# Attention and gated feed-forward on one core: weights and v as casting transfers, smaller opening loads, a first weight block done unit by unit

## The chip, the cores and the metric

The kernel runs on one core of one Trainium2 chip. The metric is the device time of one execution in microseconds (us). A profile comes from one single execution of a kernel, and its span is some 1.8 us shorter than the device time of that execution.

## The reference, cut to what matters

```python
def _attn_ref(q, k, v):                    # 8 x 8 x 576 x 64, float32
    rel = pos[:, None] - pos[None, :]
    mask = (rel >= 0) & (rel < 64)         # each query sees itself and 63 keys before it
    scores = np.where(mask, q @ k^T / sqrt(64), -1e9)
    return softmax(scores) @ v

def _moe_ref(x, w_gate, w_val, w_out):     # 4608 x 512; 512 x 1536 twice; 1536 x 512
    return (np.maximum(x @ w_gate, 0) * (x @ w_val)) @ w_out
```

x is the attention's output, 4608 tokens of 512 values. The kernel cuts the tokens into 24 **units** of 192 (three to a batch) and into 12 **tiles** of two units each. A tile goes through w_gate and w_val (the matmuls called h, in 12 column groups f = 0 to 11 each) and then through w_out (the matmuls called op). The weights are cut into three **blocks**: gate 0, 1, 2 and value 0, 1, 2, each 512 x 512, or 1 MB in float32. Block 0 serves f = 0 to 3, block 1 f = 4 to 7, block 2 f = 8 to 11.

## The kernel before

All inputs come as float32 and are computed in fp16. Before, the loads go through the sync engine's queue into float32 buffers (half of batch 0's q and k go through ScalarE's queue, before the change and after it), and GpSimd casts them in SBUF:

```python
def w_load(wt, src, j, at):
    ...
    stg = stage.tile([128, 2, 512], FP32, name="stg")
    nc.sync.dma_start(stg, part)
    def cast():
        nc.gpsimd.tensor_copy(dst, stg)
        w_done.add((wt.name, j))
    W.at(at, cast)

def v_load(u):
    ...
    nc.sync.dma_start(vn[p0:128, w], v[b, :, k0 + p0:k0 + 128].rearrange("h p d -> p h d"))

def u_cast(u, name):          # k, q and v of one unit; q of unit 0 on ScalarE, the rest on GpSimd
    ...
    nc.gpsimd.tensor_copy(c16, src)
```

`W` is a list of pieces of work with planned times; it decides only the order in which instructions are written to each engine. At run time every engine takes its own instructions in that order and waits on semaphores. The steps of one unit, in its own names:

```python
def u_exp(u, g):   ... nc.scalar.activation(p, st, ACT.Exp, scale=scale)            # ScalarE
def u_mask(u, g):  ... nc.vector.tensor_tensor(p, p, mask.to_broadcast(...), MUL)   # VectorE, two SBUF inputs
def u_copy(u, g):  ... nc.scalar.copy(d["xs"][:, g], d["pv"][g])                    # ScalarE
def u_norm(u):     ... nc.vector.tensor_tensor(xt[...], d["xs"][:, :, 0], rs, MUL)  # writes one unit's half of xt
```

The main program:

```python
        qk_load(0)                        # q and k of batch 0: units 0, 1 and 2
        ...
        W.advance(22.0)
        heat = f_ps.tile([128, 512], FP32, name="heat", tag="h")
        for _ in range(14): ...           # matmuls whose result nobody reads, to warm the clock
        ...
        ready(2)                          # units 0 and 1 normalised
        hidden(0, 0, TT)                  # h of tile 0, both units at once: 384 columns a matmul
        ready(3)
        hidden(1, 0, U)                   # h of tile 1, first unit
        output_by_rows(0)
        ...
```

The softmax here doesn't subtract the row's maximum and nothing guards it: scores larger than these inputs give would overflow.

## Time and profile before

| | before |
|---|---|
| device time, median of 3 (lowest to highest) | 362.14 us (361.67 to 362.98) |
| first h matmul | 31.93 us |
| first group that needs value block 2 (f = 8) | 45.74 us |
| first op matmul | 58.71 us |
| TensorE busy between 100 and 350 us | 249.2 of 250 us |

The table is to be read from the bottom. From about 60 us on TensorE is full, so the program's end is the moment at which that full stretch begins, plus a constant. All that moving loads and casts can gain lies in the first 60 us. I use the third row as a milestone: the start of the first h group that needs value block 2. The profile's lines that carry this stand in the prediction below, except the milestone's own:

```profile
45.74 0.81 PE L341 MATMUL h<-xt,wv 128*128 128x384 f16 x4
```

### The profile page before, as it was taken

The numbers are of one execution on the slowest core, as the hardware profiler recorded it, in microseconds if no ns is written. First come the engines' busy times: TensorE is split into PE (matmuls) and PEld (weight loads), VectorE is DVE, ScalarE is ACT, GpSimd is POOL, SyncE is SP. The second block draws the span as 40 slices with busy tenths as digits, with TensorE's granted clock in tenths as the row PEclk, the third lists the DMA queues.
The fourth block names the chain that finished last, engine by engine and source line by source line (L and its number), as shares of the span: only waits on it lengthen the run. The fifth ranks groups of instructions, "written<-read, shape, count | busy, mean of one in ns | idle before, by whom it ended". The sixth has DMA issues, their size and how long they took to land.

```text
span 360.2 us, 8167 instructions
## 1 busy us (share of the span) xinstructions
PE 333.6 (93%) x3230; PEld 196.6 (55%) x3230; DVE 238.2 (66%) x450; ACT 179.4 (50%) x387; POOL 94.7 (26%) x114
## 2 busy tenths in 40 slices
PE   0276999999999999999999999999999999999995
PEld 0253676685664664664664654654664664654652
DVE  0799747887785785776776776776686686684330
ACT  1362544674663663662662662652752752762421
POOL 2678633408115111025105210025105201000000
PEclk9998999999999999999999999999999999999999
DMA  8999948996991701991991701991992701001002
GB/s 191 262 340 388 321 122 192 208 240 152 211 183 61 148 0 60 211 184 59 217 181 59 147 2 58 204 189 64 194 195 68 147 2 58 31 2 59 31 1 87
DMA packets 94215, 49.82 MB, mean 138 GB/s; under 512 B 48096, under 2 KB 84960, under 8 KB 94176
## 3 DMA queue, kind: packets, MB, share of 16 engines
q1 hardware_dynamic: 91808, 48.12, 61.1%
q10 hardware_dynamic: 2368, 1.18, 1.5%
q8 instruction: 25, 0.41, 0.5%
q14 instruction: 14, 0.11, 0.1%
HBM read 39.85 MB, written 9.44 MB: 137 GB/s over the span
## 4 chain that ended last, share of the span: by engine, by line
PE 86%; DVE 8%; DMA 3%; ACT 1%; issue 1%; ACTq 0%; DVEq 0%
PE h L341 51%; PE op L355 25%; PE pv L253 6%; PE st L226 3%; DMA qn<-in_q_dram 3%; DVE p L242 2%; DVE xt L285 1%; DVE rs L279 1%; DVE g_sb L331 1%; DVE sT L271 1%; DVE qT L212 1%; ACT xs L266 0%; ACTq L164 0%; DVE kT L212 0%; DVE rT L273 0%
## 5 line engine op out<-in xcount | busy, mean ns | idle before, releaser
L341 PE MATMUL h<-xt,wg 128*128 128x384 f16 (+1 forms) x624 | 120.4, 316 | 3.7 <-DVE xt L285 3.5
L341 PE MATMUL h<-xt,wv 128*128 128x384 f16 (+1 forms) x624 | 120.1, 316 | 0.4 <-DVE g_sb L331 0.4
L331 DVE TENSOR_TENSOR g_sb<-r_sb,h 128x384 f16<-128x384 f32 (+1 forms) x156 | 79.1, 512 | 61.9 <-PE h L341 55.0
L328 ACT ACTIVATE r_sb<-h 128x384 f32<-128x384 f32 (+1 forms) x156 | 73.5, 472 | 77.1 <-PE h L341 53.0
L355 PE MATMUL op<-wo,g_sb 128*128 128x512 f16 x432 | 95.7, 380 | 0.0
L341 PEld LDWEIGHTS <-wg 128*128 128x128 f16 x624 | 58.8, 98 | 40.0 <-POOL wv L134 3.3
L341 PEld LDWEIGHTS <-wv 128*128 128x128 f16 x624 | 58.5, 98 | 34.7 <-issue 1.1
L355 PEld LDWEIGHTS <-g_sb 128*128 128x128 f16 x432 | 41.8, 98 | 48.9
L242 DVE TENSOR_TENSOR p<-p,mask 128x512 f16<-128x512 f16 x96 | 46.2, 503 | 30.3 <-ACT p L238 29.4
L238 ACT ACTIVATE p<-st 128x512 f16<-128x512 f32 x96 | 52.7, 611 | 9.6 <-PE st L226 9.2
L362 ACT COPY o_sb<-op 128x512 f32<-128x512 f32 x36 | 20.9, 586 | 68.6 <-PE op L355 68.6
L266 ACT COPY xs<-pv 128x384 f32<-128x384 f32 x96 | 40.2, 496 | 10.9 <-PE pv L253 10.9
L200 POOL CAST k<-kn 128x768 f16<-128x768 f32 x24 | 23.8, 992 | 77.0 <-DMA kn<-in_k_dram 44.1
L200 POOL CAST q<-qn 128x768 f16<-128x768 f32 x23 | 19.4, 843 | 56.4 <-DMA qn<-in_q_dram 42.0
L212 DVE STREAM_TRANSPOSE kT<-k 128x384 f16<-128x384 f16 x48 | 27.8, 590 | 9.0 <-POOL k L200 7.7
L193 POOL CAST v<-vn 128x1024 f16<-128x1024 f32 x16 | 16.8, 1051 | 61.7 <-PE pv L253 49.5
L226 PE MATMUL st<-qT,kT 32*128 32x128 f16 x768 | 16.9, 227 | 15.5 <-DVE qT L212 15.5
L253 PE MATMUL pv<-p,v 128*64 128x128 f16 x384 | 25.0, 229 | 3.5 <-DVE p L242 3.3
L212 DVE STREAM_TRANSPOSE qT<-q 128x384 f16<-128x384 f16 x48 | 26.5, 581 | 1.7 <-ACT q L198 1.5
L271 DVE STREAM_TRANSPOSE sT<-xs 128x768 f32<-128x768 f32 x24 | 22.7, 948 | 6.1 <-ACT xs L266 6.1
L226 PEld LDWEIGHTS <-kT 32*128 32x128 f16 x768 | 12.3, 98 | 23.3 <-issue 11.3
L253 PE MATMUL pv<-p,ones 128*64 128x128 f16 x384 | 24.5, 227 | 0.0
(28 smaller groups left out, 132.7 us busy)
## 6 DMA issues: line engine op xcount, KB each, us to landing
vn<-in_v_dram SPq DMA_DIRECT2D x40, 256.0 KB, 5.1
out_dram<-o_sb SPq DMA_DIRECT2D x36, 256.0 KB, 2.0
kn<-in_k_dram SPq DMA_DIRECT2D x26, 288.0 KB, 6.2
qn<-in_q_dram SPq DMA_DIRECT2D x26, 288.0 KB, 9.2
stg<-in_moe_w_gate_dram SPq DMA_DIRECT2D x6, 512.0 KB, 7.3
stg<-in_moe_w_val_dram SPq DMA_DIRECT2D x6, 512.0 KB, 7.0
stg<-in_moe_w_out_dram SPq DMA_DIRECT2D x6, 512.0 KB, 7.3
vn<-in_v_dram SPq DMA_DIRECT2D x8, 128.0 KB, 8.4
```

The lines of the kernel that those rows point to most:

```text
L200: nc.gpsimd.tensor_copy(c16, src)
L212: nc.vector.transpose(dst.rearrange("p h (m i j) -> p h m j i", i=32, j=2), src)
L226: nc.tensor.matmul(d["st"][g][:, (2 * hh + w) * 128:(2 * hh + w + 1) * 128], kT[rows, dh, hh, ks + 128 * w:ks + 128 * w + 128], d["qT"][ro ...
L238: nc.scalar.activation(d["p"][g].rearrange("p h c -> p (h c)"), d["st"][g], ACT.Exp, scale=scale)
L242: nc.vector.tensor_tensor(p, p, mask.rearrange("p w c -> p (w c)")[:, None, :].to_broadcast([128, 2, 256]), MUL)
L253: nc.tensor.matmul(pv[64 * e:64 * e + 64, s, 64 * w:64 * w + 128], d["v16"][:, w, 2 * g + e] if s == 0 else (ones0 if u % UB == 0 and w == ...
L266: nc.scalar.copy(d["xs"][:, g], d["pv"][g])
L271: nc.vector.transpose(sT.rearrange("p g b c -> p g (b c)"), d["xs"][:, :, 1])
L328: nc.scalar.activation(r_sb[:, 0:n], h1[:, 0:n], ACT.Relu)
L331: nc.vector.tensor_tensor(g_sb[:, f, c0:c1], r_sb[:, 0:n], h2[:, 0:n], MUL)
L341: nc.tensor.matmul(h[:, 0:n], wt[:, c, f * 128:f * 128 + 128], xt[:, c, c0:c1], start=(c == 0), stop=(c == NC - 1))
L355: nc.tensor.matmul(op, g_sb[:, f, bass.ds(sub * 128, 128)], wo[:, f], start=(f == 0), stop=(f == NF - 1))
```

## The change

Its intent is to get TensorE going earlier. It has three parts, which I call a, b and c.

- **a** Weights and v are cast on their way in. A transfer issued from GpSimd reads float32 and writes fp16. The float32 buffers and GpSimd's casts of weights and v go away; GpSimd now issues those transfers instead. The sync engine's queue keeps q, k and the outputs.
- **b** The opening loads of q and k cover units 0 and 1 only; unit 2's part follows later.
- **c** Weight block 0 is applied to unit 0 as soon as that is ready, then to unit 1 (192 columns a matmul), and only from f = 4 on to both at once. The heating matmuls are gone.

```diff
-        stg = stage.tile([128, 2, 512], FP32, name="stg")
-        nc.sync.dma_start(stg, part)
-        def cast(): nc.gpsimd.tensor_copy(dst, stg) ...
+        nc.gpsimd.dma_start(dst, part)                      # a: casts on the way
 ...
-            nc.sync.dma_start(vn[p0:128, w], v[b, ...])
+            nc.gpsimd.dma_start(v16[p0:128, w], v[b, ...])  # a
 ...
-        qk_load(0)
+        qk_load(0, (0, 6), "k", True)                       # b: units 0 and 1
+        qk_load(0, (0, 6), "q", True)
 ...
+        W.at(6.5, lambda: v_load(0))
+        W.at(9.8, lambda: v_load(1))
+        cols = [(wt, src, j) for j in range(3) for wt, src in ((wg, moe_w_gate), (wv, moe_w_val))]
+        rows = [(wo, moe_w_out, j) for j in range(3)]
+        for c, t in zip(cols + rows, (8.0, 12.0, 16.0, 19.0, 25.0, 28.0, 34.0, 37.0, 40.0)):
+            W.at(t, lambda c=c: w_load(*c))
+        W.at(9.0, lambda: qk_load(0, (6, 9)))               # b: unit 2
+        W.at(22.0, lambda: v_load(2))
+        W.at(31.0, lambda: qk_load(1, (0, 3)))
 ...
+        plan_unit(2, 26.0, (16.0, 17.0), ...)               # unit 2's k and q casts on GpSimd
 ...
-        for _ in range(14): ... heat ...
-        hidden(0, 0, TT)
+        ready(1)
+        hidden(0, 0, U, 0, 4)                               # c
+        ready(2)
+        hidden(0, U, TT, 0, 4)
+        hidden(0, 0, TT, 4)
```

(Cut: plan times of the other units, helper arguments, the casts of unit 0's k and unit 1's q moved from GpSimd to ScalarE, and the weights' transfers, which read 1 MB each instead of 512 KB.)

More of the change, by code (lines that the diff above doesn't have):

```diff
@@ L70 @@
     persist = ctx.enter_context(tc.tile_pool(name="persist", bufs=1))
-    stage = ctx.enter_context(tc.tile_pool(name="stage", bufs=6))
     a_in = ctx.enter_context(tc.tile_pool(name="a_in", bufs=2))
@@ L120, with w_load @@
     w_done = set()
-    def w_load(wt, src, j, at):
+    def w_load(wt, src, j):
         sr = src.rearrange("(c p) n -> p c n", p=128)
         if wt is wo:
-            dst, part = wo[:, 2 * j:2 * j + 2], sr[:, 2 * j:2 * j + 2]
+            dst, part = wo[:, 4 * j:4 * j + 4], sr[:, 4 * j:4 * j + 4]
         else:
-            cs, ns = slice(2 * (j % 2), 2 * (j % 2) + 2), slice(512 * (j // 2), 512 * (j // 2) + 512)
-            dst, part = wt[:, cs, ns], sr[:, cs, ns]
-        stg = stage.tile([128, 2, 512], FP32, name="stg")
-        nc.sync.dma_start(stg, part)
-        def cast():
-            nc.gpsimd.tensor_copy(dst, stg)
-            w_done.add((wt.name, j))
-        W.at(at, cast)
+            ns = slice(512 * j, 512 * j + 512)
+            dst, part = wt[:, :, ns], sr[:, :, ns]
+        nc.gpsimd.dma_start(dst, part)
+        w_done.add((wt.name, j))
     def w_need(wt, f):
-        j = f // 2 if wt is wo else 2 * (f // 4) + 1
-        while (wt.name, j) not in w_done:
+        while (wt.name, f // 4) not in w_done:
             W.pop()
-    def queue(b, g):
-        return nc.scalar if b == 0 and g >= G // 2 else nc.sync
     def qk_tiles(b):
@@ L154, in qk_tiles, with qk_load @@
                 units[UB * b + i][name + "nat"] = nat
-    def qk_load(b, blocks=None):
+    def qk_load(b, blocks=None, names="kq", two=False):
         for name, src in (("k", k), ("q", q)):
+            if name not in names:
+                continue
             nat = units[UB * b + UB - 1][name + "nat"].rearrange("p h u m e -> p h (u m) e")
@@ L162, in qk_load @@
                 rows = slice(32 * g, 32 * g + 32)
+                eng = nc.scalar if two and g >= G // 2 else nc.sync
                 if blocks is None:
-                    queue(b, g).dma_start(
+                    eng.dma_start(
                         nat[rows].rearrange("p h m e -> p (h m) e"),
@@ L169, in qk_load @@
                     for h in range(2):
-                        queue(b, g).dma_start(
+                        eng.dma_start(
                             nat[rows, h, m0:m1],
@@ L177, in v_load @@
         d = units[u]
-        vn = d["v"] = a_in.tile([128, 2, H, 64], FP32, name="vn", bufs=3)
+        v16 = d["v16"] = a_16.tile([128, 2, H, 64], FP16, name="v16", bufs=3)
+        if u == 0:
+            nc.vector.memset(v16[0:64, 0], 0.0)
+        elif uu == 0:
+            nc.gpsimd.memset(v16[0:64, 0], 0.0)
         for w in range(2):
@@ L181, in v_load @@
             p0 = max(0, -k0)
-            nc.sync.dma_start(vn[p0:128, w], v[b, :, k0 + p0:k0 + 128].rearrange("h p d -> p h d"))
+            nc.gpsimd.dma_start(v16[p0:128, w], v[b, :, k0 + p0:k0 + 128].rearrange("h p d -> p h d"))
     def u_cast(u, name):
         d = units[u]
-        if name == "v":
-            v16 = d["v16"] = a_16.tile([128, 2, H, 64], FP16, name="v16")
-            if u % UB == 0:
-                nc.gpsimd.memset(v16[0:64, 0], 0.0)
-                nc.gpsimd.tensor_copy(v16[64:128, 0], d["v"][64:128, 0])
-                nc.gpsimd.tensor_copy(v16[:, 1], d["v"][:, 1])
-            else:
-                nc.gpsimd.tensor_copy(v16, d["v"])
-        else:
-            c16 = d[name + "16"] = a_16.tile([128, 2, 3, 128], FP16, name=name + "16")
-            src = d[name]
-            if name == "q" and u == 0:
-                nc.scalar.copy(c16, src)
-            else:
-                nc.gpsimd.tensor_copy(c16, src)
+        c16 = d[name + "16"] = a_16.tile([128, 2, 3, 128], FP16, name=name + "16")
+        src = d[name]
+        if u < 2 and (u, name) != (1, "k"):
+            nc.scalar.copy(c16, src)
+        else:
+            nc.gpsimd.tensor_copy(c16, src)
     def u_trans(u, name, dh):
@@ L295, in plan_unit @@
             W.at(T - 20, lambda: v_load(u))
-        cast = cast or (T - 11, T - 10, T - 9)
+        cast = cast or (T - 11, T - 10)
         tr = tr or (T - 6.8, T - 3.4)
-        for name, t in zip(("k", "q", "v"), cast):
+        for name, t in zip(("k", "q"), cast):
             W.at(t, lambda name=name: u_cast(u, name))
@@ L318, in ready, with hidden @@
             W.pop()
-    def hidden(t, c0, c1):
+    def hidden(t, c0, c1, f0=0, f1=NF):
         if t not in gs:
@@ L333, in gate @@
                 done.add(f)
-        for f in range(NF):
+        for f in range(f0, f1):
             for i, wt in enumerate((wg, wv)):
@@ L392 @@
         nc.scalar.activation(warm[:, 1:2], warm[:, 0:1], ACT.Exp)
-        v_load(0)
-        v_load(1)
+        qk_load(0, (0, 6), "q", True)
         constants()
-        chunks = [(wt, src, 2 * j + i) for j in range(3)
-                  for wt, src in ((wg, moe_w_gate), (wv, moe_w_val)) for i in range(2)]
-        chunks += [(wo, moe_w_out, j) for j in range(6)]
-        t_load, t_land = 6.0, 17.5
-        for i, c in enumerate(chunks):
-            if i == 4:
-                W.at(t_load, lambda: v_load(2))
-                t_load, t_land = t_load + 2.4, t_land + 2.4
-            W.at(t_load, lambda c=c, at=t_land: w_load(*c, at))
-            t_load, t_land = t_load + 1.4, t_land + 1.4
@@ L406 @@
-        W.at(t_load, lambda: qk_tiles(1))
-        W.at(t_load, lambda: qk_load(1, (0, 3)))
-        W.at(t_load, lambda: v_load(3))
-        W.at(t_load + 5.0, lambda: qk_load(1, (3, 9)))
-        W.at(t_load + 5.0, lambda: v_load(4))
-        W.at(t_load + 5.0, lambda: v_load(5))
-        plan_unit(0, 12.0, (6.0, 10.0, 11.7), (7.0, 10.5), 0.8, 1.4, 3.6, 4.7, 6.2, 0.5)
-        plan_unit(1, 13.0, (6.8, 10.1, 12.7), (8.0, 12.0), 1.8, 2.4, 4.5, 5.2, 8.1, 0.5)
-        plan_unit(2, 18.3, (7.6, 10.9, 24.5), (9.0, 12.8), 1.6, 5.5, 8.0, 9.0, 10.4, 0.4)
@@ L415 @@
-        plan_unit(3, 50.0, (44.0, 46.5, 47.5), (45.5, 48.2), 0.8, 1.5, 3.4, 4.5, 6.4, 0.5)
-        plan_unit(4, 58.0)
-        plan_unit(5, 66.0)
-        W.advance(22.0)
-        heat = f_ps.tile([128, 512], FP32, name="heat", tag="h")
-        for _ in range(14):
-            nc.tensor.matmul(heat[:, 0:256], mask[:, 0], mask.rearrange("p w c -> p (w c)"),
-                             start=True, stop=True)
-        W.advance(24.0)
-        T = 78.0
+        W.at(6.5, lambda: v_load(0))
+        W.at(9.8, lambda: v_load(1))
@@ new lines @@
+        cols = [(wt, src, j) for j in range(3) for wt, src in ((wg, moe_w_gate), (wv, moe_w_val))]
[4 more added lines that the diff above has]
+        W.at(22.0, lambda: v_load(2))
+        W.at(10.0, lambda: qk_tiles(1))
+        W.at(31.0, lambda: qk_load(1, (0, 3)))
+        W.at(31.0, lambda: v_load(3))
@@ new lines @@
+        W.at(42.0, lambda: qk_load(1, (3, 9)))
+        W.at(42.0, lambda: v_load(4))
+        W.at(45.0, lambda: v_load(5))
+        plan_unit(0, 10.0, (5.5, 8.3), (6.2, 9.0), 0.8, 1.4, 3.2, 4.2, 5.8, 0.5)
+        plan_unit(1, 11.0, (5.6, 9.1), (7.1, 9.9), 1.9, 2.4, 4.3, 5.0, 7.2, 0.5)
+        plan_unit(2, 26.0, (16.0, 17.0), (22.5, 24.0), 0.8, 1.5, 3.4, 4.5, 6.4, 0.5)
+        plan_unit(3, 43.0, (36.0, 37.0), (38.0, 40.0), 0.8, 1.5, 3.4, 4.5, 6.4, 0.5)
+        plan_unit(4, 55.5)
+        plan_unit(5, 63.3)
@@ L425 @@
+        T = 75.6
         for t in range(3, NU // 2):
@@ L427 @@
             plan_unit(2 * t + 1, T + 13.2)
-            T += 27.0
+            T += 27.125
+        W.advance(20.3)
+        ready(1)
+        hidden(0, 0, U, 0, 4)
         ready(2)
-        hidden(0, 0, TT)
+        hidden(0, U, TT, 0, 4)
+        hidden(0, 0, TT, 4)
         ready(3)
```

## The prediction

> **What bounds the kernel now.** I read the busy shares first, then the 40 slices, then the chain of waits over the first 60 us, then the timeline of each engine there. The lines from the page:
>
> ```profile
> PE 333.6 (93%) x3230; PEld 196.6 (55%) x3230; DVE 238.2 (66%) x450; ACT 179.4 (50%) x387; POOL 94.7 (26%) x114
> ...
> PE   0276999999999999999999999999999999999995
> ...
> DMA  8999948996991701991991701991992701001002
> GB/s 191 262 340 388 321 122 192 208 240 152 211 183 61 148 0 60 211 184 59 217 181 59 147 2 58 204 189 64 194 195 68 147 2 58 31 2 59 31 1 87
> ```
>
> TensorE is full from the fifth slice (9 us each) to the end; in 100 to 350 us it is busy 249.2 of 250. That stretch can't be shortened by moving casts and loads. What can move is when TensorE becomes full. The chain shows what holds it back:
>
> ```profile
> 2.41 10.46 DMA qn<-in_q_dram
> ...
> 13.03 0.84 ACT q L198
> ...
> 17.20 7.24 DVE p L242 x8
> 24.44 0.90 DVE sT L271
> ...
> 29.95 1.85 DVE xt L285
> 31.79 0.14 issue
> 31.93 4.36 PE h L341 x16
> 36.28 1.01 PE pv L253 x32
> 37.30 17.79 PE h L341 x136
> ```
>
> Columns: start us, length us, what. Reading it: until 12.87 us everything waits for q to land; then eight mask multiplies on VectorE take 7.24 us; then the two units' normalisations follow one another on VectorE to 31.79 us; only then does the first hidden-layer matmul (h) start, and its first 16 run slowly. From 37.3 us on TensorE is the chain. Two timeline lines show why the masks are slow and why the first matmuls are:
>
> ```profile
> 17.09 7.35 DVE L242 TENSOR_TENSOR p<-p,mask 128x512 f16<-128x512 f16 x8
> 19.08 2.40 POOL L134 CAST wg<-stg 128x1024 f16<-128x1024 f32 x2
> 31.93 1.44 PE L341 MATMUL h<-xt,wg 128*128 128x384 f16 x4 [3.02 <-DVE xt L285]
> 37.23 0.82 PE L341 MATMUL h<-xt,wg 128*128 128x384 f16 x4
> ```
>
> GpSimd casts back to back beside the masks. A mask takes 0.92 us here, while the median of all 96 is 0.422 us. A group of four h matmuls takes 1.44 us at first; later they start every 0.65 us.
>
> [...] 0.92 against 0.42 us, and an xt multiply of 1.84 us beside weight casts against 0.96 without. [...] Before, nearly everything is on one queue (q1, 48.12 of 49.82 MB), so the sharing is unseen too. [...] h groups take 1.44, 1.49, 1.19 and then 0.81 us.
>
> **The change part by part.**
>
> *Removed from GpSimd:* 18 weight casts (7.1 + 7.0 + 6.2 = 20.3 us) and the v casts (16.8 + 5.1 + 4.9 = 26.8 us). GpSimd is at 26%, so this is worth nothing by itself; it counts through the masks. Eight masks at 0.42 instead of 0.92 us save 4.0 us of VectorE. But the exponentials then set the pace, so the gain has to be built up along the chain.
>
> *The opening loads:* q and k of batch 0 are 2.36 MB, and q had landed at 12.87 us. Now units 0 and 1 alone need 1.57 MB. Adding up the rates of the first 20 us in half-us steps (about 190 to 340 GB/s), 1.58 MB had moved by 8.5 us. So q lands near 8.7 us, 4 us earlier. The instruction order shows q's loads waiting for the semaphores of k's and the k cast of unit 0 behind them on ScalarE; I put that cast near 6.5 us, early enough. Before, q's cast started at 13.03 and the first exponential at 15.95, 2.9 us later. ScalarE now casts two units' q, but unit 0 first. First exponential: about 11.8 us.
>
> *From there to the first h:* ScalarE's order is eight exponentials (4.0 us) and unit 0's four copies (1.9 us), giving 17.8 us. Unit 0's transpose, reciprocal, transpose and multiply took 3.3 us before (24.36 to 27.67), so its half of x is ready at about 21.2 us, the other half 3.3 us later at 24.5 us. The first weight block is now done unit by unit, so TensorE starts at 21.2 instead of 31.9 us.
>
> *TensorE's opening:* sixteen groups of 192 columns (eight per unit) at 0.33 us are 2 x 2.6 us, the same work as eight groups of 384. The 14 heating matmuls are gone and the clock is cold again: I add 1.8 us. Block 0 is then complete at about 28.3 us. Unit 2's scores and values, done in or before this stretch in the old kernel, come afterwards: 0.6 + 1.0 us. Before, group f=4 started at 39.84 us with all this behind it; now it corresponds to 28.3 + 1.6 = 29.9 us. **Gain before any weight wait: 9.9 us.**
>
> *The weights:* block 1 is needed at about 28 us and block 2 at about 35 us. A block pair is 2.1 MB, 5.4 us at the 387 GB/s that the slices show for weights alone. GpSimd's queue has, in order, v0, gate 0, v1, value 0, gate 1, casts of unit 2's k and q, value 1, v2, gate 2, value 2. At 387 GB/s for weights and about 210 for v (estimates from the trace's rates, assuming casting costs nothing) these are 22.8 us of transfer up to value 2. From 8.3 us, alone, they would be there at 31 us, in time. But the sync engine no longer paces itself by weights: nothing holds its q and k loads of batches 0, 1 and 2 back but their predecessors and free buffers, so they run ahead and share the engines. If a 2 KB weight packet (85 ns at 387/16 GB/s) alternates with a 512 B q/k packet (33 ns at 250/16), weights get 72% of the time: value 1 at 29 us, value 2 at 40 us. Against 28.3 and about 35.5 this costs 0.7 and up to 4 us, overlapping in part. I take **3 us lost to waits for weights**, so a net 6.9 us.
>
> *Afterwards:* tile 1, the outputs and the 27-us rhythm have the same matmuls. GpSimd has two v issues per unit in place of casts and ample time. I expect no change there, and perhaps 0.3 us from small waits at 56 to 69 us. Sum: 362.14 - 7.1 = 355.0 us.
>
> **The rivals.**
> - *Transfers become the bound.* For it: DMA is at 9 tenths through the first five slices before, casting transfers have an unknown rate, and q/k loads run ahead. At half the weight rate (5.4 us per MB), block 2 would come near 50 us; TensorE would wait about 14 us and the change would lose about 4: 366 us. Against it: the bytes to read are the same and the bytes to write are half.
> - [...] A v transfer has 1024 pieces of 64 values. If one costs 3 us to issue, v1 and value 0 come several us late, the queue blocks in order, and the gain falls to 3 or 4 us: 358.5 us. In the steady state GpSimd has room for it.
> - *All hidden well.* If GpSimd's queue is served preferentially, block 2 is in time and the gain is 9 to 10 us: 352.5 us.
> - *The start is not what sets the end.* Units 3 to 5 could become late through GpSimd's in-order queue, giving the gain back at 50 to 80 us. Against it: before, the waits there are under 0.6 us each although the loads were queued behind all weights.
>
> **Range and chances.** Centre 355.0 us[...]. The 2% line is at 362.14 x 0.98 = 354.9, almost on the centre, so faster and same are equally likely at 0.47 each. The slow-cast case gets 0.06. Eight times in ten: 350 to 361 us.
>
> **What would show it.** In the new profile: masks of the first units at about 0.42 us; q landing near 8.7 and first exponential near 11.8 us; first h near 21 us; waits of h for weights of about 3 us in all between 24 and 42 us;[...] from 60 us on, the old timeline shifted earlier by 7 us. The prediction is wrong if h starts near 21 us and then waits over 6 us for weights (slow casting or sharing), if q still lands after 11 us (the semaphores of the eight smaller loads), if masks stay near 0.9 us[...], or if new waits of several us appear after 60 us.

Where a cut is marked, the text stated rules of the hardware, mechanisms or figures that no trace of this case had shown, or named a case after them; the figures of the trace that stood beside them are left. No term of the sum is cut; it stands as put on record, 362.14 less 7.1, 355.0 us. 1.8 us for the cold clock is an estimate; it agrees with the trace of the kernel before, where the first 16 h matmuls took 4.36 us and as many later take 4 x 0.65 us. That the packets of two queues alternate was an assumption when it was written; the counts after the change (146 and 146, below) bear it out. The numbers in the rivals (half the weight rate, 3 us to issue a v transfer) are what-ifs and were read off no trace.

## The result, and the profile after

| | before | after |
|---|---|---|
| device time, median (lowest to highest) | 362.11 us (361.67 to 362.98, 4 runs) | 357.47 us (356.0 to 358.2, 4 runs) |
| ratio after / before, 95% interval | | 0.9864 (0.9826 to 0.9902) |
| the profiled run | 361.96 us | 356.0 us |
| first h matmul | 31.93 us | 22.10 us |
| first group that needs value block 2 | 45.74 us | 40.20 us |
| first op matmul | 58.71 us | 54.83 us |

A ratio here and below is the mean time of one kernel's fast runs over the mean of the other kernel's fast runs of the same rounds, so it isn't quite the ratio of the medians quoted beside it. The change is 1.4% faster, which is inside the 2% line. Note that the profiled run is the fastest of the four.

The page of the changed kernel, its totals and two of its slice rows (40 slices, 9 us each):

```profile
PE 331.8 (94%) x3248; PEld 198.3 (56%) x3248; DVE 230.3 (65%) x455; ACT 181.9 (51%) x393; POOL 92.8 (26%) x118
...
PE   0469899999999999999999999999999999999995
...
PEclk9958999999999999999999999999999999999999
DMA  6999999959944417958956406967986311001002
```

TensorE fills up one slice earlier, but the third slice stands at a granted clock of 0.5 and the fifth at only 8 tenths busy. The transfers are at 9 tenths from the second slice through the eighth, longer than before. GpSimd is as busy as before (26%): the casts were replaced by issuing.

The chain of waits of the changed kernel, its part from 10 to 45 us (start us, length us, what):

```profile
10.46 6.82 DMA kn<-in_k_dram
...
17.65 5.76 DMA kn<-in_k_dram
23.41 0.81 POOL q L188
...
24.91 1.76 POOL v L179 x2
26.67 0.62 POOL wg L129
...
27.38 12.78 DMA wv<-in_moe_w_val_dram
...
40.20 4.81 PE h L329 x29
```

Read from the bottom: the h group at 40.20 us waited for value block 2, whose transfer took 12.78 us. It was issued at 27.38 us because it stood behind other issues on GpSimd; those stood behind a cast of unit 2's q; and that cast waited until 23.41 us for unit 2's q and k, loads that have nothing to do with weights. GpSimd's own timeline shows the same head of line (start us, length us, then the idle time before the instruction and its releaser in brackets):

```profile
12.23 0.80 POOL L129 DMA_DIRECT2D wg<-in_moe_w_gate_dram  x1
17.43 1.03 POOL L188 CAST k<-kn 128x768 f16<-128x768 f32 x1 [4.40 <-ACT p L226]
23.39 0.83 POOL L188 CAST q<-qn 128x768 f16<-128x768 f32 x1 [4.93 <-DMA kn<-in_k_dram]
24.16 0.74 POOL L129 DMA_DIRECT2D wv<-in_moe_w_val_dram  x1
```

From 13.0 to 24.2 us GpSimd issues nothing. TensorE in the changed kernel:

```profile
22.10 0.82 PE L329 MATMUL h<-xt,wg 128*128 128x192 f16 x4
23.63 0.82 PE L329 MATMUL h<-xt,wv 128*128 128x192 f16 x4 [0.70 <-DMA wv<-in_moe_w_val_dram]
...
28.72 0.65 PE L329 MATMUL h<-xt,wv 128*128 128x192 f16 x4
29.21 0.49 PE L329 MATMUL h<-xt,wg 128*128 128x192 f16 x4
...
31.19 0.81 PE L329 MATMUL h<-xt,wg 128*128 128x384 f16 x4
...
40.20 0.82 PE L329 MATMUL h<-xt,wv 128*128 128x384 f16 x4 [1.22 <-DMA wv<-in_moe_w_val_dram]
```

The sixteen groups of block 0 take from 22.10 to 31.19 us, 9.09 us. At full clock they start every 0.33 us, 5.28 us in all; 0.70 us is the wait for value 0, and the remaining 3.1 us is the cold clock (granted 0.50 from 24 to 28.7 us), which lasts until 28.7 us. Then comes the wait for value 2: without it the group would have started at 38.83 us (one group of 0.65 us after the one at 38.18 us), so it cost 1.37 us.

How the two queues shared the engines shows in one microsecond in which both were full, 22 to 23 us (packets, MB written, share of the engines' time; packets overlap in time, so the shares add up to over 100%):

```profile
q0 software_dynamic: 146, 0.15, 87.6%
q1 hardware_dynamic: 146, 0.07, 34.4%
```

q0 carries the casting transfers, q1 the sync engine's q and k. In these stretches they moved packet for packet: 146 to 146 here, and 280 to 280 from 36 to 38 us.

### The profile page after: what moved, and what is told of

Read it like the earlier page. It is cut to its first block, busy times and chain, and to the rows that moved or that the text cites. A ratio compares the mean times of both kernels' runs of the same rounds, so it can differ in the third digit from the quotient of the medians.

```text
span 354.2 us, 8180 instructions
## 1 busy us (share of the span) xinstructions
PE 331.8 (94%) x3248; PEld 198.3 (56%) x3248; DVE 230.3 (65%) x455; ACT 181.9 (51%) x393; POOL 92.8 (26%) x118
## 4 chain that ended last, share of the span: by engine, by line
PE 85%; DMA 9%; DVE 2%; POOL 1%; ACT 1%; SPq 0%; issue 0%; ACTq 0%; POOLq 0%
PE h L329 51%; PE op L343 25%; PE pv L241 6%; DMA kn<-in_k_dram 5%; DMA wv<-in_moe_w_val_dram 4%; PE st L214 3%; DMA qn<-in_q_dram 1%; DVE sT L259 1%; DVE rs L267 1%; POOL v L179 0%; ACT xs L254 0%; SPq L163 0%; ACTq L163 0%; DVE xt L273 0%; POOL q L188 0%
## 5 line engine op out<-in xcount | busy, mean ns | idle before, releaser
L329 PE MATMUL h<-xt,wv 128*128 128x384 f16 (+1 forms) x640 | 121.6, 314 | 2.3 <-DMA wv<-in_moe_w_val_dram 1.9
L329 PE MATMUL h<-xt,wg 128*128 128x384 f16 (+1 forms) x640 | 121.8, 314 | 0.2 <-DVE xt L273 0.2
L316 ACT ACTIVATE r_sb<-h 128x384 f32<-128x384 f32 (+1 forms) x160 | 74.3, 466 | 69.1 <-PE h L329 54.5
L343 PE MATMUL op<-wo,g_sb 128*128 128x512 f16 x432 | 96.9, 379 | 0.0
L329 PEld LDWEIGHTS <-wv 128*128 128x128 f16 x640 | 61.1, 99 | 36.4 <-DMA wv<-in_moe_w_val_dram 2.7
L329 PEld LDWEIGHTS <-wg 128*128 128x128 f16 x640 | 60.7, 99 | 36.0 <-issue 2.4
L179 POOL DMA_DIRECT2D v<-in_v_dram x48 | 40.7, 856 | 33.0 <-PE pv L241 33.0
L230 DVE TENSOR_TENSOR p<-p,mask 128x512 f16<-128x512 f16 x96 | 40.7, 450 | 12.3 <-ACT p L226 11.7
L188 POOL CAST k<-kn 128x768 f16<-128x768 f32 x23 | 22.1, 960 | 67.6 <-DMA kn<-in_k_dram 19.7
L214 PE MATMUL st<-qT,kT 32*128 32x128 f16 x768 | 16.4, 223 | 11.7 <-DVE qT L200 11.7
L241 PEld LDWEIGHTS <-v 128*64 128x64 f16 x384 | 16.7, 113 | 12.7 <-issue 7.9
```

What stands on the lines that cost most here:

```text
L179: nc.gpsimd.dma_start(v16[p0:128, w], v[b, :, k0 + p0:k0 + 128].rearrange("h p d -> p h d"))
L214: nc.tensor.matmul(d["st"][g][:, (2 * hh + w) * 128:(2 * hh + w + 1) * 128], kT[rows, dh, hh, ks + 128 * w:ks + 128 * w + 128], d["qT"][ro ...
L230: nc.vector.tensor_tensor(p, p, mask.rearrange("p w c -> p (w c)")[:, None, :].to_broadcast([128, 2, 256]), MUL)
L241: nc.tensor.matmul(pv[64 * e:64 * e + 64, s, 64 * w:64 * w + 128], d["v16"][:, w, 2 * g + e] if s == 0 else (ones0 if u % UB == 0 and w == ...
L316: nc.scalar.activation(r_sb[:, 0:n], h1[:, 0:n], ACT.Relu)
L329: nc.tensor.matmul(h[:, 0:n], wt[:, c, f * 128:f * 128 + 128], xt[:, c, c0:c1], start=(c == 0), stop=(c == NC - 1))
```

## The experiments

My theory after this reading: **the landing of the last weight block in GpSimd's queue (value 2, at 40 us) sets the end of the program, and how early TensorE starts hardly matters**. The rivals: the start sets the end (then c is what pays, and the cold clock is what spoils it), or something later does. Eleven variants were run on three chips, each with runs of the kernel before on the same chip (medians there 362.15, 362.45 and 362.43 us), and the changed kernel itself was run once more, on a fourth (362.04 us).

| run | what it is | median us | ratio to before (95%) | value-2 group starts |
|---|---|---|---|---|
| e1_joint_block | c undone | 356.17 | 0.9821 (0.9797, 0.9845) | 40.48 |
| e2_heat | heating added | 357.99 | 0.9873 (0.9841, 0.9906) | 40.38 |
| e3_value1_first | GpSimd's order mended for value 1 | 357.04 | 0.9851 (0.9827, 0.9875) | 40.79 |
| e4_paced | batch 1's loads held back | 361.28 | 0.9971 (0.9946, 0.9996) | 38.81 |
| e5_weights_early | all weights ahead of unit 2's casts and v2 | 363.87 | 1.0018 (0.9992, 1.0044) | 47.71 |
| e6_early_paced | e5 and batch 1 held back | 358.61 | 0.9864 (0.9833, 0.9895) | 43.94 |
| e7_early_paced_heat | e6 and heating | 357.10 | 0.9844 (0.9817, 0.9870) | 42.20 |
| e8_whole_open | b undone | 360.28 | 0.9927 (0.9903, 0.9951) | 43.20 |
| e9_supply | order of need, and batch 1 held back | 353.70 | 0.9753 (0.9722, 0.9783) | 37.37 |
| e10_supply_heat | e9 and heating | 353.15 | 0.9746 (0.9719, 0.9774) | 35.91 |
| e11_supply_joint | e9 with c undone | 356.44 | 0.9825 (0.9795, 0.9855) | 40.07 |
| e12_after_again | the changed kernel | 357.97 | 0.9878 (0.9843, 0.9914) | 41.34 |

All gave the reference's result.

### e1: does the early start pay? (part c undone)

```diff
-        ready(1)
-        hidden(0, 0, U, 0, 4)
         ready(2)
-        hidden(0, U, TT, 0, 4)
-        hidden(0, 0, TT, 4)
+        hidden(0, 0, TT)
```

> The changed kernel with tile 0's first weight block done jointly again, as before the change: the first hidden matmul waits for both units. Theory of the prediction (the start of h sets the end, and unit by unit brings it forward): in the changed kernel the first h began at 22.1 us and unit 1's x was ready at 26.05; so h starts near 26.1 here, runs eight groups of 384 partly at the cold clock, and block 1 is reached some 2 to 3 us later than at 31.2 us: about 359.5 us. Rival (the weights of the value matrix set the pace, their last wait ends at 40.2 us whatever goes before): the slack before value 1 and value 2 absorbs it, and the time stays within 1 us of 357.5.

TensorE in this run:

```profile
25.37 1.44 PE L329 MATMUL h<-xt,wg 128*128 128x384 f16 x4 [4.03 <-DVE xt L273]
...
32.42 0.81 PE L329 MATMUL h<-xt,wg 128*128 128x384 f16 x4
```

h starts 3.3 us later than in the change, yet f = 4 is reached at 32.42 instead of 31.19 us, because the groups are never held up by value 0 and pass fewer of their columns through the cold clock (three slow groups, the first of 1.44 us; granted 0.50 from 24 to 28 us). At f = 8 it doesn't wait at all: it gets there at 40.48 us, after value 2. The run is no slower than the changed kernel, 356.17 us; the intervals of their ratios just overlap. With e12's second set of runs of the change (0.9878) beside the first (0.9864), e1's 0.9821 lies some 0.5% lower: 1.8 us, with an interval of about 0.5 to 3.1 us, which is an estimate, as the sets ran on different chips. So in the change as it stands part c is worth nothing, and more likely costs a little. The early start is spent waiting. The rival had the direction right; its range ended at 356.5 us, 0.3 us above the median.

### e2: does the cold clock cost anything? (heating added)

```diff
+        def heat(n): ...   # n matmuls of 256 columns on the mask, result unread
+        W.at(14.0, lambda: heat(20))
```

> The changed kernel with 20 heating matmuls put between unit 0's and unit 1's values product, where TensorE idled from 15.9 to 19.2 us. Theory (ten groups of h cost 0.64 instead of 0.33 us at the half clock, 3.1 us in all): h groups of 192 columns run every 0.33 us from the start, block 1 is reached about 3 us earlier. Rival (weights set the pace): value 1, which was issued only at 24.2 us because GpSimd's queue stood behind the cast of unit 2's q, lands near 31 to 32 us, so h waits there and then again for value 2 at 40.2 us; the time then falls by under 1 us. First theory alone: about 354.5 us. Rival: 356.5 to 357.5 us, with new waits for the value weights of 2 to 3 us.

TensorE in this run:

```profile
21.66 0.49 PE L329 MATMUL h<-xt,wg 128*128 128x192 f16 x4 [1.33 <-DVE xt L273]
...
40.38 1.46 PE L329 MATMUL h<-xt,wv 128*128 128x384 f16 x4 [2.76 <-DMA wv<-in_moe_w_val_dram]
41.63 1.49 PE L329 MATMUL h<-xt,wg 128*128 128x384 f16 x4
```

The heating works: the groups run at 0.33 us from the first one, where nothing holds them up, and f = 4 starts at 28.65, 2.5 us earlier than in the change. It gains nothing, because value 2 comes at 40.38 us all the same. Worse, after the longer wait (2.76 us) the clock is down, 0.83 on the mean of 40 to 50 us, and the groups there take 1.46 and 1.49 us instead of 0.82. Being earlier at a closed door isn't merely useless: in this profile it has a price of 1.5 us, which the rival's 356.5 to 357.5 us didn't have. The medians of e2 and the change (357.99 and 357.47 us) don't differ clear of noise.

### e3: is it GpSimd's order? (value 1 ahead of unit 2's casts)

```diff
-        W.at(22.0, lambda: v_load(2))
+        W.at(19.1, lambda: v_load(2))
-        plan_unit(2, 26.0, (16.0, 17.0), ...)
+        plan_unit(2, 26.0, (19.2, 19.6), ...)
```

> The changed kernel with unit 2's k and q casts put behind value 1 and v2 in GpSimd's in-order queue, nothing else. In the changed kernel GpSimd stood from 18.5 to 23.4 us for unit 2's q, value 1 was issued at 24.2, and the transfer rate dipped to some 75 to 175 GB/s between 23 and 27 us. Theory (that blocking delays value 1 and 2): value 1 is issued near 13 us, the dip goes, value 2 lands before 38.8 us, the 1.2 us wait at 40.2 us goes: about 356.2 us. Rival (the DMA engines are full anyway, and the run-ahead of the q and k loads decides): value 2 still lands near 40 us, time 357.5 us.

Value 1 was issued at 12.65 instead of 24.16 us, and the dip in the transfers between 24 and 27 us was gone. But the wait for value 2 stayed:

```profile
40.79 0.82 PE L329 MATMUL h<-xt,wv 128*128 128x384 f16 x4 [1.73 <-DMA wv<-in_moe_w_val_dram]
```

Gate 2 and value 2 still stood behind the q cast (issued at 24.57 and 25.32 us), and the engines were full from 16 to 44 us (210 GB/s up to 26 us, 207 from 24 us on): the sync engine's q and k of later batches took the room that had been freed. This much order alone does nothing. My expectation was wrong and the rival's right.

### e4: is it the sync engine running ahead? (batch 1's loads held back)

Two tiny memsets on VectorE write into the buffers that the loads of batch 1 fill, so the loads must wait for VectorE to get there.

```diff
+        W.at(28.0, lambda: hold(0)); W.at(42.0, lambda: hold(3))   # nc.vector.memset(nat[:, 0, m, 0:1], 0.0)
-        W.at(31.0, lambda: qk_load(1, (0, 3)))
+        W.at(28.0, lambda: qk_load(1, (0, 3)))                     # (3, 9) at 42.0 as before, behind its hold
-        ... (8.0, 12.0, 16.0, 19.0, 25.0, 28.0, 34.0, 37.0, 40.0)
+        ... (8.0, 12.0, 16.0, 19.0, 25.0, 28.0, 34.0, 35.0, 35.5)  # w_out's blocks close together
```

> The changed kernel with batch 1's q and k loads held back by a tiny write into their tile (one at the plan's 28 us, one at 42 us), so that the sync engine can't run ahead of the weights; the three output weight blocks are issued together. Theory (q and k loads that run ahead take engine time from the weights): between 18 and 32 us the weights have the engines alone, value 2 lands several us before 38.8 us, its wait goes, time about 356 us. Rival (GpSimd's queue order decides, since value 2 was issued only at 27.4 us, or casting transfers are slow by themselves): value 2 still takes over 9 us from issue and the wait stays, 357.5 us.

Value 2 was used at 38.81 us, only 1.4 us earlier, and the run lost nearly everything: 361.28 us, far from both expectations. Two things explain it. From 24 to 27 us the engines stood nearly idle (28, 1 and 32 GB/s in the three microseconds), because value 1 was still behind the q cast on GpSimd (issued at 24.80 us) and nothing else was left to move. And batch 1 now came too late: VectorE waited 4.03 us for the cast of unit 3's q (until 50.02 us), the gating multiplies stood behind that in its order, and TensorE waited 3.70 us for those:

```profile
51.36 0.49 PE L329 MATMUL h<-xt,wg 128*128 128x192 f16 x4 [3.70 <-DVE g_sb L319]
```

After that wait h groups of 0.49 us took 0.76 to 0.85 us from 52.34 to 55.88 us; the granted clock was 0.83 on the mean of 50 to 60 us. Taking competitors away from a queue that wasn't filled gained nothing here. The run does give one clean number, a stretch in which casting weights move alone, 32 to 35 us:

```profile
q0 software_dynamic: 608, 0.61, 122.1%
```

A weight packet writes 512 fp16 values (0.61 MB in 608 packets) and reads the same values in float32, 2 KB; 15 of the 608 packets are under 512 B and carry no weights. The other 593 in 3 us are 198 a microsecond, or 405 GB/s of reading. The kernel before read weights at 389 GB/s (25 to 30 us). In this stretch, casting on the way cost no rate.

### e5, e6, e7: the weights first

e5 puts value 1, gate 2, value 2 and v2 before unit 2's casts, e6 adds one hold of batch 1 at plan time 24, e7 adds e2's heating.

```diff
-        ... (8.0, 12.0, 16.0, 19.0, 25.0, 28.0, 34.0, 37.0, 40.0)
+        ... (8.0, 12.0, 16.0, 19.0, 19.1, 19.2, 34.0, 37.0, 40.0)
-        W.at(22.0, lambda: v_load(2))
+        W.at(19.4, lambda: v_load(2))
-        plan_unit(2, 26.0, (16.0, 17.0), ...)
+        plan_unit(2, 26.0, (19.8, 19.9), ...)
+        W.at(24.0, hold)                           # e6, e7; the loads of batch 1 follow at 24.0
+        W.at(14.0, lambda: heat(20))               # e7
```

> The changed kernel with value 1, gate 2, value 2 and v2 all issued before unit 2's k and q casts on GpSimd; the sync engine's loads run ahead as in the changed kernel. Theory (value 2's landing sets the end; in the changed kernel it came at 40.16 us, in the heated one at 40.38, in the one with value 1 first at 40.79): with its place in the ring moved forward past v2 it lands 1.5 to 3 us earlier even though weights and q/k packets alternate, at 37 to 39 us, the wait of 1.2 us goes: about 356.0 us. Rival (another bound just behind): no change, 357.5 us.

> As the run with early weights, and batch 1's q and k loads are held back once, by a tiny VectorE write in the plan's order between unit 2's k and q transposes (about 29 us). Theory: between 18 and 29 us the weights have the engines alone at about 400 GB/s read, value 2 lands near 33 us, no wait for weights is left; but the cold clock stays, so block 1 is still reached at 31 us and the time is about 356 us. Rival (holding back delays batch 1, as in the paced run, where unit 3's casts came at 43 and 49 us): a wait before unit 3, 358 us or more.

> As the last, plus the 20 heating matmuls. If the cold clock and the late value weights are the two reasons why the earlier start was not worth its 9.9 us, each hiding the other, then only taking away both shows it: h from 21.7 us at 0.33 us a group, block 1 near 28.7 us, block 2 near 35.5 us without wait: about 353.5 us. If the time is above 356 us, a third bound exists and must be looked for in the waits.

The wait for value 2 is gone in all three, and another has taken its place. In e5:

```profile
40.01 0.32 PE L241 MATMUL pv<-p,v 128*64 128x128 f16 x2 [6.36 <-DMA v<-in_v_dram]
41.40 0.32 PE L241 MATMUL pv<-p,v 128*64 128x128 f16 x2 [1.08 <-DMA v<-in_v_dram]
```

v2 is now last in the queue, lands at 40 us, and unit 2's value product stands in the middle of f = 6 in TensorE's order. e5 is no faster than the kernel before. With batch 1 held (e6) v2 costs 2.19 + 0.96 us, with heating (e7) 0.71 + 1.17 us. In e7's profile the heating didn't even hold: after a wait of 0.98 us for value 0 the groups start every 0.64 us from 24.2 to 26.8 us, and f = 4 comes at 30.80 us, later than e6's 30.03. I had mended the order by looking at the one wait that the profile showed, and had put the next needed thing last. With the engines shared, what stood last in the queue came near 40 us, v2 here (40.01 us) as value 2 in the change (40.16 us); only its name had changed. e5 and e6, on one chip, size the hold under this order: 5.3 us (363.87 less 358.61). e6's 358 us or more had been expected too, but from a late batch 1; the cause was v2.

### e8: what is part b worth? (the opening loads whole)

```diff
-        qk_load(0, (0, 6), "k", True)
+        qk_load(0, None, "k", True)                # the same for "q"
-        W.at(9.0, lambda: qk_load(0, (6, 9)))
```

> The changed kernel with the opening q and k loads of batch 0 whole again, as in the kernel before. Theory of the prediction (2.36 instead of 1.57 MB ahead of q's landing): q's cast begins near 13 instead of 10 us, first h about 3 us later, near 25 us; but value 2, which in the changed kernel lands at 40.2 us whatever comes before, hides most of it, since unit 2's casts no longer hold GpSimd's queue: 357 to 359 us. If the start set the end: 360.5 us.

360.28 us, outside my 357 to 359 us and next to the 360.5 us of the rival that the start sets the end. The trace speaks against that rival:

```profile
43.20 1.46 PE L329 MATMUL h<-xt,wv 128*128 128x384 f16 x4 [2.89 <-DMA wv<-in_moe_w_val_dram]
```

ScalarE's first q cast starts at 13.52 us instead of 9.99, the first h at 25.48 instead of 22.10, but TensorE still gets to value 2 too early, waits 2.89 us for it until 43.20 us, and has a cold clock behind it (groups of 1.46 and 1.49 us). Value 2 was issued at 20.01 us, 7.4 us before the change did, and still landed 3 us later; GpSimd's first transfer went out at 9.61 instead of 7.33 us. So b is worth some 2.8 us of medians (360.28 less 357.47; 2.3 us by the ratios), not because h starts earlier but because value 2 lands earlier. The run also sizes the masks: unit 0's half of x is ready 9.0 us after its first exponential (16.44 to 25.4 us), 8.9 us in the changed kernel (12.91 to 21.81), and 11.7 us in the kernel before (15.95 to 27.67).

### e9: both ends of the supply together

GpSimd issues in the order in which TensorE needs things (value 1, v2, gate 2, value 2, then unit 2's casts), and batch 1 is held once, at plan time 24.

```diff
-        ... (8.0, 12.0, 16.0, 19.0, 25.0, 28.0, 34.0, 37.0, 40.0)
+        ... (8.0, 12.0, 16.0, 19.0, 19.1, 19.2, 34.0, 37.0, 40.0)
-        W.at(22.0, lambda: v_load(2))
+        W.at(19.05, lambda: v_load(2))             # e5 to e7: 19.4, behind value 2
-        plan_unit(2, 26.0, (16.0, 17.0), ...)
+        plan_unit(2, 26.0, (19.8, 19.9), ...)
+        W.at(24.0, hold)                           # qk_load(1, (0, 3)) follows at 24.0
```

> Both limits on the weights' supply taken away in the order in which TensorE needs the data: value 1, v2, gate 2, value 2 are issued ahead of unit 2's casts, and batch 1's q and k loads are held back once (as in the sixth run). Clock as in the changed kernel. Theory (whatever is last in GpSimd's ring by 40 us sets the pace; the last runs showed v2 in that place at 37 to 40 us): v2 lands near 30, value 2 near 36 us; block 1 is reached at 31.2 us as in the changed kernel and nothing waits after it: 356.0 us. Rival (the order is worthless, the ring is full in any order): some wait of 1 us or more for v2 or a weight block stays, 357.5 us.

TensorE in this run:

```profile
23.40 0.82 PE L329 MATMUL h<-xt,wv 128*128 128x192 f16 x4 [0.34 <-DMA wv<-in_moe_w_val_dram]
...
29.73 0.81 PE L329 MATMUL h<-xt,wg 128*128 128x384 f16 x4
...
37.37 0.81 PE L329 MATMUL h<-xt,wv 128*128 128x384 f16 x4
```

After 23.40 us no h group and no value product waits for a transfer. Value 2 is issued at 19.72 instead of 27.38 us and is there in time. It could have gone out earlier still: the trace shows GpSimd, with ten transfers issued, waiting 2.00 us for gate 0 to land before it issues gate 2. The median is 353.70 us, 2.5% below the kernel before and clearly under the changed kernel: its interval ends at 0.9783, below where that of the change begins (0.9826). So order and hold together give 3.8 us more than the change, where part of the order (e3) had given nothing and another hold (e4) a loss. They aren't exact halves: e3 left gate 2 and value 2 behind the casts, and e4 held back at other times and moved w_out; e9's order without its hold and its hold without its order weren't run. Against e6, the nearest run, only v2's place differs: 4.9 us of medians (358.61 less 353.70, on different chips). This version beats both kernels. It also beat its expectation of 356.0 us: f = 4 starts at 29.73 instead of the 31.2 us expected, since the clock was warm from 24.6 us on (groups at 0.33 us). In the profiles that is half of e9's lead of 2.8 us at the milestone, and it is chance, as e12 shows: there the changed kernel itself got to f = 4 at 29.67 us.

### e10 and e11: heating and unit by unit, with the supply in order

> As the last run, plus the 20 heating matmuls, which were worth nothing where value 2 landed at 40.4 us. Theory: block 1 is reached near 28.5 us, then waits of at most 1 us for value 2 near 36 us: about 354 us. Rival (heating is worth nothing in any case): as the last run.

> As the ninth run, with block 1 of the weights (the first four row groups) done for both units jointly again. Where the supply set the pace, joint and unit by unit were alike (356.2 and 357.5 us). If the supply no longer does, the 3 us later start of h shows, less the time at the cold clock that both pay: 1 to 2 us more than the ninth run. If they are alike again, unit by unit is worth nothing because the cold clock eats it.

e10 is e9 with e2's heating: 353.15 us, the same within the intervals. The value-2 group starts 1.5 us earlier than in e9's profile, and the end is 0.4 us earlier in the spans (351.3 and 351.7 us). The rest is given back later: TensorE waits 0.48 us at 50.80 us for ScalarE's copies and 0.92 us at 74.63 us for a mask, where e9 has one wait of 0.33 us, at 80.62 us. In e9's profiled run the clock happened to be warm without any heating, so the two profiles don't size the heating; the medians do.

e11 is e9 with part c undone, the edit of e1: 356.44 us.

```profile
40.07 0.81 PE L329 MATMUL h<-xt,wv 128*128 128x384 f16 x4
```

So with the supply in order c is worth 2.7 us (356.44 less 353.70; I had expected 1 to 2), and the milestone shows the same 2.7 us (40.07 less 37.37). In e1, under the old supply, it was worth nothing or less. The same edit has two different values, depending on whether another limit lies right behind it.

### e12: the changed kernel again, and a rule

> The changed kernel itself, unedited, run a second time with more rounds. Two things are tested. (1) A rule read off the profiled runs so far: the device time is 316 us plus the start of the first group of h matmuls that needs value block 2 (before 45.74 and 361.96, after 40.20 and 356.0, the early-weights run 47.71 and 364.01, the supply run 37.37 and 353.59), as long as the clock stays warm after that group; if the group waits some 2.8 us and runs cold (1.46 us instead of 0.82) the rule is 316 plus 1.7. If the landing of the last weight block sets the end, the new profiled run obeys the rule within 0.6 us whatever its time is. The rival, that the spread of 356.0 to 358.2 us comes from later in the program, expects a run of 357 to 358 us with that group still at 40.2 us. (2) The size of the gain: theory expects a ratio of 0.986 (0.983 to 0.989) once more, a median of 356.5 to 358; the rival, that the first four runs drew badly and the change is as fast as the joint-block run, expects 0.982 and a median near 356.

By then the profiled runs suggested a rule: device time = start of the value-2 group + a constant. The new profiled run tested it, and missed it as it was written; it is still the most telling profile of all, because it's a bad one (360.47 us, the range being 355.88 to 360.47). TensorE in it:

```profile
29.67 0.81 PE L329 MATMUL h<-xt,wg 128*128 128x384 f16 x4
...
37.79 0.82 PE L329 MATMUL h<-xt,wg 128*128 128x384 f16 x4 [0.80 <-DMA wg<-in_moe_w_gate_dram]
41.34 1.46 PE L329 MATMUL h<-xt,wv 128*128 128x384 f16 x4 [2.72 <-DMA wv<-in_moe_w_val_dram]
42.59 1.49 PE L329 MATMUL h<-xt,wg 128*128 128x384 f16 x4
```

The clock warmed earlier here (groups at 0.33 us from 26.4 us on), so f = 4 starts at 29.67, 1.5 us **earlier** than in the first profile. Yet the run ends 4.5 us **later**. The q cast on GpSimd came 0.9 us later, value 2 was issued at 28.25 and landed at 41.29 us. TensorE had arrived so early that its wait was 2.72 us; the clock fell (groups of 1.46 and 1.49 us); and five groups took 5.91 us (41.34 to 47.25) instead of 3.25. By the rule, 316 us plus 1.7 where the group runs cold, this run should have taken 359.0 us. It took 1.4 us more, outside the 0.6 us that I had allowed: 1.7 was too small a cold term for it. The table has the rule over all profiled runs with the cold excess measured in each run, a correction made after the result. The excess is that kind of difference (5.91 less 3.25), counted over the groups that follow the wait:

| run | group starts | device time | difference | cold excess | difference less excess |
|---|---|---|---|---|---|
| before | 45.74 | 361.96 | 316.2 | 0 | 316.2 |
| after | 40.20 | 356.00 | 315.8 | 0 | 315.8 |
| e12 | 41.34 | 360.47 | 319.1 | 2.7 | 316.5 |
| e1 | 40.48 | 356.53 | 316.1 | 0 | 316.1 |
| e2 | 40.38 | 358.27 | 317.9 | 1.5 | 316.4 |
| e3 | 40.79 | 357.04 | 316.3 | 0 | 316.3 |
| e5 | 47.71 | 364.01 | 316.3 | 0 | 316.3 |
| e6 | 43.94 | 359.67 | 315.7 | 0 | 315.7 |
| e7 | 42.20 | 358.54 | 316.3 | 0 | 316.3 |
| e8 | 43.20 | 360.96 | 317.8 | 1.3 | 316.5 |
| e9 | 37.37 | 353.59 | 316.2 | 0 | 316.2 |
| e10 | 35.91 | 353.00 | 317.1 | 0 | 317.1 |
| e11 | 40.07 | 356.86 | 316.8 | 0 | 316.8 |
| e4 | 38.81 | 360.82 | 322.0 | 0 | 322.0 |

Twelve of fourteen lie between 315.7 and 316.8 us. e4 stands out by its late batch 1 (the wait of 3.70 us at 51.36 us is over half of it, and the cold clock after it follows), e10 by the two small waits named above. So from that group on the profiled runs differ by little but the cold clock right behind it, in every kernel but those two. It isn't always value 2 that starts the group: in the kernel before, e1, e5 to e7, e9 and e11 TensorE came to it after value 2 had landed, and in e10 just as it landed. Of the 4.5 us between the two profiles of the change, the later group is 1.1 and the cold clock behind it 2.7; the rival that I wrote down for this run, a cause later in the program, is left with 0.7 us.

The second part of the expectation held: 357.97 us, ratio 0.9878, in the range the theory gave.

## Why the prediction was right or wrong, point by point

The time fell inside the range, 2.5 us above the centre, and the change is within 2%, which was one of two classes held equally likely. The mechanism was right: TensorE starts earlier by the masks and the smaller loads, part of that is lost to weights because the sync engine runs ahead, and nothing changes afterwards. Two of its sizes were wrong, and in the first profile their errors partly cancelled: 9.9 less 3 us were forecast, 7.0 less 1.4 measured. (The forecast's own sum is off as well: 6.9 and 0.3 us make 7.2, not 7.1.) Its terms:

- **"q lands near 8.7 us", "first exponential: about 11.8 us".** 1.1 us too early. ScalarE's q cast began at 9.99 us, the first exponential at 12.91 us.
- **Masks at 0.42 us.** Right. The first seven masks took 3.36 us, 0.48 each (one alone 0.42), with GpSimd idle. The eighth, at 17.35 us, took 0.42 us although a cast on GpSimd began beside it; that cast took 1.03 instead of 0.83 us. From the first exponential to unit 0's x I had 9.4 us; it was 8.9. Nor did issuing slow VectorE where the trace shows both: an xt multiply (25.09 us) took 0.96 us while GpSimd issued v transfers, the time it takes undisturbed.
- **"TensorE starts at 21.2".** 22.10, late by what q was late.
- **"The clock is cold again: I add 1.8 us."** Mis-sized: 3.1 us in the first profile, and the cost varied from run to run. The clock was full 5.1 us after the wait for value 0 in the first profile, 3.1 us after it in the second (23.25 to 26.37) and 1.2 us in e9 (23.40 to 24.59).
- **"Gain before any weight wait: 9.9 us."** This is the term that failed. It was 7.0: f = 4 at 31.19 plus 1.6 us for unit 2's work that still follows is 32.8, against 39.84 before. The missing 2.9 us are 0.9 (h later), 1.3 (colder) and 0.7 (the wait for value 0, which I'd counted nowhere).
- **"3 us lost to waits for weights."** The waits were predicted well: value 2 at 40 us, measured 40.16; the weights' share 72%, measured 146 packets a microsecond of the 198 that they reach alone, 74%. That 40 us came out so closely is partly luck, as the reckoning had no standing queue (next point); but e3, without that stand, used value 2 at 40.79 us. The cost was 1.4 us at value 2 in the first profile, and 2.7 + 0.8 us with 2.7 us of cold clock behind them in the second. That after a wait of 2.72 us the clock was down again was in no step of mine. It is most of the difference between the two profiled runs, of which the first gained 6.0 us on the profiled run of before and the second 1.5; the median's gain of 4.6 us lies between them. What the unprofiled runs met isn't known.
- **The order on GpSimd.** I listed "gate 1, casts of unit 2's k and q, value 1" and reckoned the queue as if it were always full. It stood from 13.0 to 17.4 us for unit 2's k and from 18.5 to 23.4 us for its q. e3 shows that this alone cost nothing, since the sync engine filled the room; e9 shows that the order as a whole and the running ahead together cost 3.8 us.
- **"Afterwards ... no change there."** Right: 316.2 us follow the milestone before the change, and 315.8 and (less the cold excess) 316.5 us with it.
- **The rivals.** Slow casting transfers: wrong, 405 GB/s read. Slow issuing on GpSimd: wrong, 0.86 us per v transfer, 0.75 to 0.80 per weight block. All hidden: wrong for this kernel; e9 is what it would look like, and at 353.7 us it comes near the 352.5 that I gave for it. The start isn't what sets the end: right in its headline, though not through units 3 to 5 as I wrote but through value 2.

What stays open: why value 2's landing itself varies (40.16 and 41.29 us in two profiles of one kernel; the q cast on GpSimd differed by 0.9 us, and I have not traced it further), and whether e1 is truly faster than the change, as the estimate under e1 suggests. Part a was never undone by itself, nor were the transfers of 1 MB and the casts moved to ScalarE, so what each of them is worth alone isn't shown.

## What to carry to other kernels

Before speeding up what comes before a wait, look at what lands last there and when: time gained ahead of it was lost again here, and the longer idle stretch was followed by a cold clock on top (1.5 us in e2, 1.3 in e8, 2.7 in e12). Moving loads to a second queue also took the brake off the first one here (the sync engine issued batch 1's first loads at 17.65 us, 38.20 before), so order each queue by when its contents are needed and hold back what isn't needed yet; here an order mended in part gave nothing (e3), a hold beside the old order a loss (e4), and the full order with a hold 3.8 us. When an edit measures as zero, that is its value under the present limit: try it again when that limit has gone (part c: nothing or less, then 2.7 us).

## What these runs show of transfers and the clock

- Weights, cast on the way and alone on the engines, came at 198 packets of 2 KB a microsecond, 405 GB/s of reading (e4, 32 to 35 us), against 389 GB/s for plain float32 loads in the kernel before (25 to 30 us).
- An issue on GpSimd took 0.75 to 0.80 us for a weight block (512 pieces of 2 KB) and 0.86 us for a v transfer (1024 pieces of 256 B).
- From 22 to 23 us of the changed kernel the two queues moved 146 packets each, although one's were of 2 KB read and the other's of 512 B. The queue with the small ones got the smaller part of the bytes (0.07 MB written against 0.15) but as many packets.
- In e4, into idle engines, value 1 was issued at 24.80 us and the first packets moved at about 26.2 us, 1.4 us later (0.7 us after the issue had ended); from 27 to 28 us the engines still moved only 113 GB/s.
- In these runs no single length of wait decided whether the clock fell: the groups ran cold after waits of 2.72, 2.76 and 2.89 us (e12, e2, e8), but also in e7 after waits of 0.67 and 0.98 us (0.64 us a group instead of 0.33), while after the waits for value 2 of 1.22 to 1.73 us in the change, e3 and e4 they ran at full pace (0.82 us). What separates these cases isn't shown; no experiment set the waits on purpose.
